# A gated linear recurrence and an MLP in one kernel: blocks of four chunks, a token permutation by DMA, wider FF1 products, a new program order

## The chip, the cores and the metric

The kernel runs on one core of a Trainium2 chip. The metric is the device time of one execution in microseconds; the median of three runs of the kernel before is 198.5 us (196.85 to 198.63).

## The reference

A recurrence over 768 tokens, for 4 batches and 8 heads of 48 channels, followed by an MLP whose activation is h cos(h):

```python
# q, k, v, alpha: (4, 8, 768, 48) f32;  w_in: (384, 2048), w_out: (2048, 384) f32
for t in range(S):
    state = alpha[:, :, t, :, None] * state + np.einsum('bhd,bhe->bhde', k[:, :, t], v[:, :, t])
    y[:, :, t] = np.einsum('bhd,bhde->bhe', q[:, :, t], state)
x = y.transpose(0, 2, 1, 3).reshape(B * S, H * D)      # 3072 x 384
h = x @ w_in
out = (h * np.cos(h)) @ w_out                           # 3072 x 384 f32
```

## The kernel before

The 3072 tokens are 24 chunks of 128, six to a batch; a token is a partition. For a chunk `j`, the logarithms of alpha (`ln`, ACT, L144) are summed along the tokens by a product with a triangular matrix (`cums`, PE, L157), four small products give the sums of the whole chunk (L161), and two exponentials give the decay of each token from the chunk's start and its inverse (`exps`, ACT, L175, L177). These work on pairs of chunks, except for the first two. k is multiplied by the inverse decay (`khat`, POOL, L185), q by the decay (`qhat`, POOL, L191), v is cast (`vcast`, POOL, L195). k and q go, transposed, into the scores (`scores`, PE, L235), which are masked (`mask_scores`, DVE, L244). The transposes are made on PE for the first 8 chunks (`transposes`, L218, evicted by DVE, L224), and by a transposing DMA from SBUF to SBUF for the others (L211). The state is a product of k and v (`state`, PE, L260), to which DVE adds the former state (L272) and which POOL multiplies by the chunk's decay (L274, into `ub`). `outputs` (L289, L292) adds q times state and scores times v; DVE evicts y as bf16 (`ev_outputs`, L299); `x_transposes` turns it, on PE for 6 chunks (L313) and by a transposing DMA for the rest (L307).

The MLP works on one chunk and half of the 2048 hidden channels at a time: FF1 (`ff1`, L330) is 8 x 3 products of 128 x 128 x 128 into a PSUM tile of two banks; ACT takes the cosine as a shifted sine (`act`, L338), DVE multiplies (`gate`, L344), FF2 (`ff2`, L352) adds 2 x 8 products with 384 columns, ACT evicts (L357) and sends the result out on its own DMA queue. `warmup` (L368) issues products of zeros.

All loads and all transposing DMAs are issued by SP, in program order. A load is one chunk of one tensor: 8 heads x 128 tokens, 192 bytes contiguous each (L100, L104). The weights come in quarters of 768 KB (L111, L124), and are cast by DVE and ACT (L117, L115). PSUM has three double-bank buffers (`big`, for sums, scores and FF1), one bank `g` (transposes, state, outputs) and one bank `o` (FF2).

The scheduler is off: a string `ORDER` of 678 units is the program, and each engine takes its instructions in that order. A unit is a letter and a chunk, for example `v0 b0 a0 a1 i0 c0 k0 d0`.

Of the kernel before, what the change touches and what calls it, by code (L numbers as in the profile page):

```python
# [9 lines left out]
FP = mybir.dt.float32  # L10
BF = mybir.dt.bfloat16
# [5 lines left out]
def kernel(  # L17
# [17 lines left out]
    NF = DF // C  # L35
    HF = NF // 2
    HD = H * D
    TD = 8
    QB = 6
    XD = 6  # L40
    CW = HD + NP
    ACOL = [(h % 2) * NP + h // 2 for h in range(H)]
    PF = 6

    consts = ctx.enter_context(tc.tile_pool(name="consts", bufs=1))
    apool = ctx.enter_context(tc.tile_pool(name="apool", bufs=4))
    inpool = ctx.enter_context(tc.tile_pool(name="inpool", bufs=PF))
    cpool = ctx.enter_context(tc.tile_pool(name="cpool", bufs=4))
# [3 lines left out]

# [6 lines left out]
    triu_bf = consts.tile([C, C], BF, tag="triu_bf")  # L59
    make_upper_triangular(nc, triu_bf, 1.0, diag=True)  # L60
    ones_bf = consts.tile([C, 1], BF, tag="ones_bf")
    nc.vector.memset(ones_bf, 1.0)
    halfpi = consts.tile([C, 1], FP, tag="halfpi")
    nc.vector.memset(halfpi, math.pi / 2.0)
    lnab = consts.tile([C, 2, 2, H, 64], BF, tag="lnab")
    nc.vector.memset(lnab, 0.0)
    ident_bf = consts.tile([C, C], BF, tag="ident_bf")
    make_identity(nc, ident_bf)
    kqb = consts.tile([C, 3, 2, H, 64], BF, tag="kqb")
    nc.vector.memset(kqb, 0.0)  # L70
    khb, qhb = kqb[:, :, 0], kqb[:, :, 1]


    vpb = consts.tile([C, 3, H, D], BF, tag="vpb")

    ub = consts.tile([C, 3, NP, 96], BF, tag="ub")
    nc.vector.memset(ub, 0.0)
    mask_f = consts.tile([C, C], FP, tag="mask_f")
    make_upper_triangular(nc, mask_f, 1.0, diag=True)
# [3 lines left out]
    nc.vector.memset(m2[64:128, 1:2], 1.0)  # L83

    w1f = consts.tile([C, 3, DF], FP, tag="w1f")
    w1 = consts.tile([C, 3, DF], BF, tag="w1")
    w2f = consts.tile([C, NF, DM], FP, tag="w2f")
    w2 = consts.tile([C, NF, DM], BF, tag="w2")

    a_t, q_t, k_t, v_t, cp_t, icp_t = {}, {}, {}, {}, {}, {}  # L90

    def rows(t, j):
        b, c = j // NC, j % NC
        return t[b, :, c * C : (c + 1) * C, :].rearrange("h s d -> s h d")

    def load_a(j):
        if j % 2 == 0:
            a_new = apool.tile([C, 2, H, D], FP, tag="a_sb")
            a_t[j // 2] = a_new
        nc.sync.dma_start(out=a_t[j // 2][:, j % 2], in_=rows(alpha, j))  # L100

    def load(nm, src, d, j):
        t = inpool.tile([C, H, D], FP, tag=nm)
        nc.sync.dma_start(out=t, in_=rows(src, j))  # L104
        d[j] = t

    QF = DF // 4

    def load_w1(h):
        f = slice(h * QF, (h + 1) * QF)  # L110
        nc.sync.dma_start(out=w1f[:, :, f], in_=moe_w_in[:, f].rearrange("(k p) f -> p k f", p=C))  # L111
# [7 lines left out]
    def cast_w1(h, eng, k0, k1):  # L119
        f = slice(h * QF, (h + 1) * QF)  # L120
        cast(eng, w1[:, k0:k1, f], w1f[:, k0:k1, f])

    def load_w2(h):
        nc.sync.dma_start(  # L124
            out=w2f[:, 4 * h : 4 * h + 4],
            in_=moe_w_out[4 * h * C : (4 * h + 4) * C, :].rearrange("(f p) n -> p f n", p=C),
        )

    def cast_w2(h):
        cast((nc.vector, nc.scalar)[h % 2], w2[:, 4 * h : 4 * h + 4], w2f[:, 4 * h : 4 * h + 4])  # L130

# [8 lines left out]
    def ln(j0, n):  # L140
        lnset()
        g = j0 // 2
        lo = j0 % 2
        nc.scalar.activation(  # L144
            out=lnab[:, g % 2, lo : lo + n, :, 0:D], in_=a_t[g][:, lo : lo + n], func=AF.Ln
        )

    cum_ps = {}

    def cums(j0, n):  # L150
        g = j0 // 2
        lo = j0 % 2
        if lo == 0 or n == 2:
            cum_new = ps.tile([C, 2, 512], FP, tag="big", bufs=3)
            cum_ps[g] = cum_new
        for i in range(lo, lo + n):
            nc.tensor.matmul(  # L157
                cum_ps[g][:, i, 0:HD], triu_bf, lnab[:, g % 2, i, :, 0:D], start=True, stop=True
            )
            for p in range(NP):  # L160
                nc.tensor.matmul(  # L161
                    cum_ps[g][:, i, HD + p : HD + p + 1],
                    lnab[:, g % 2, i, 2 * p : 2 * p + 2].rearrange("s h d -> s (h d)"),
                    ones_bf, start=True, stop=True,
                )

    def exps(j0, n):
        lnset()
        g = j0 // 2
        lo = j0 % 2  # L170
        if lo == 0 or n == 2:
            cp_new = cpool.tile([C, 2, CW], FP, tag="cpl")
            icp_new = cpool.tile([C, 2, HD], FP, tag="icpl")
            cp_t[g], icp_t[g] = cp_new, icp_new
        nc.scalar.activation(out=icp_t[g][:, lo : lo + n], in_=cum_ps[g][:, lo : lo + n, 0:HD],  # L175
                             func=AF.Exp, scale=-1.0)
        nc.scalar.activation(out=cp_t[g][:, lo : lo + n], in_=cum_ps[g][:, lo : lo + n, 0:CW],  # L177
                             func=AF.Exp, scale=1.0)


    Em_t = {}

    def khat(j):
        icp = icp_t[j // 2][:, j % 2]
        nc.gpsimd.tensor_tensor(out=khb[:, j % 3, :, 0:D], in0=k_t.pop(j),  # L185
                                in1=icp.rearrange("s (h d) -> s h d", h=H), op=ALU.mult)

    def qhat(j):
        cp = cp_t[j // 2][:, j % 2]
        eng = nc.vector if j < 2 else nc.gpsimd  # L190
        eng.tensor_tensor(out=qhb[:, j % 3, :, 0:D], in0=q_t.pop(j),  # L191
                          in1=cp[:, 0:HD].rearrange("s (h d) -> s h d", h=H), op=ALU.mult)

    def vcast(j):
        nc.gpsimd.tensor_copy(out=vpb[:, j % 3, :, 0:D], in_=v_t.pop(j))  # L195

    def emask(j):
        cp = cp_t[j // 2][:, j % 2]
        Em = work.tile([C, NP, 2], FP, tag="Em", bufs=3)
        nc.gpsimd.tensor_tensor(  # L200
            out=Em, in0=cp[:, HD:CW].unsqueeze(2).to_broadcast([C, NP, 2]),
            in1=m2.unsqueeze(1).to_broadcast([C, NP, 2]), op=ALU.mult,
        )
        Em_t[j] = Em

    qkT_ps, qkT_t = {}, {}

    def transposes(j):
        if j >= TD:
            t = work.tile([C, 2 * NP, C], BF, tag="qkT", bufs=QB)  # L210
            nc.sync.dma_start_transpose(out=t, in_=kqb[:, j % 3].rearrange("s i h d -> s (i h d)"))  # L211
            qkT_t[j] = t.rearrange("r b s -> r (b s)")
            return
        t = ps.tile([C, 2 * NP * C], BF, tag="g")
        qkT_ps[j] = t
        for i, src in enumerate((khb, qhb)):
            for p in range(NP):
                nc.tensor.transpose(  # L218
                    t[:, (i * NP + p) * C : (i * NP + p + 1) * C],
                    src[:, j % 3, 2 * p : 2 * p + 2].rearrange("s h d -> s (h d)"), ident_bf)  # L220

    def ev_transposes(j):
        t = work.tile([C, 2 * NP * C], BF, tag="qkT", bufs=QB)
        nc.vector.tensor_copy(out=t, in_=qkT_ps.pop(j))  # L224
        qkT_t[j] = t
# [3 lines left out]
    def scores(j):  # L229
        t = ps.tile([C, H * C], FP, tag="big", bufs=3)  # L230
        A_ps[j] = t
        for h in range(H):
            base = 64 * (h % 2)
            p = h // 2
            nc.tensor.matmul(  # L235
                t[:, ACOL[h] * C : (ACOL[h] + 1) * C],
                qkT_t[j][base : base + D, p * C : (p + 1) * C],
                qkT_t[j][base : base + D, (NP + p) * C : (NP + p + 1) * C],
                start=True, stop=True,
            )  # L240

    def mask_scores(j):
        t = work.tile([C, H * C], BF, tag="A_sb")
        nc.vector.tensor_tensor(  # L244
            out=t.rearrange("s (h t) -> s h t", h=H),
            in0=A_ps.pop(j).rearrange("s (h t) -> s h t", h=H),
            in1=mask_f.unsqueeze(1).to_broadcast([C, H, C]), op=ALU.mult,
        )
        A_t[j] = t
# [6 lines left out]
    def state(j):  # L256
        t = ps.tile([C, 512], FP, tag="g")
        U_ps[j] = t
        for p in range(NP):
            nc.tensor.matmul(  # L260
                t[:, p * 96 : (p + 1) * 96],
                khb[:, j % 3, 2 * p : 2 * p + 2].rearrange("s h d -> s (h d)"),
                vpb[:, j % 3, 2 * p : 2 * p + 2, 0:D], start=True, stop=True,
            )

    def ev_state(j):

        t = U_ps.pop(j)[:, 0 : NP * 96].rearrange("r (p e) -> r p e", p=NP)
        sc = t
        if j % NC != 0:  # L270
            sc = work.tile([C, NP, 96], FP, tag="sc")
            nc.vector.tensor_tensor(out=sc, in0=t, in1=ub[:, us(j - 1), :, 0:96], op=ALU.add)  # L272
        eng = nc.vector if j % NC == 0 else nc.gpsimd
        eng.tensor_tensor(  # L274
# [171 lines left out]
```

## Time and profile before

| | |
|---|---|
| median of three runs | 198.5 us (196.85, 198.50, 198.63) |
| span of the profiled execution, first to last instruction | 195.9 us |
| what lies around the span, against the three times | 1.0 to 2.7 us |
| mean granted TensorE clock | 1.000 |
| PE busy | 176.9 us, of it warm-ups 16.3 |
| FF1 (L330), FF2 (L352) | 70.6 us, 68.8 us |
| DVE, ACT, POOL busy | 123.6, 117.4, 75.4 us |
| DMA | 36.20 MB in 131416 packets, 124736 of them under 512 B |
| HBM read, written | 25.17 MB, 4.72 MB |
| loads of one chunk, issue to landing | 4.3 to 4.6 us |
| transposing DMAs, issue to landing | 3.9 us (x), 4.4 us (k and q) |

The profile is of one execution. Busy times of PE hold the pipeline's tails, so a group's busy time is more than the time that it takes when something follows; in the DMA row of the slices, 9 stands for 90% or more. A DMA share above 1 means that packets overlap on an engine. The windows give busy time by stretch of the span; the chain is the work that ended last, followed back.

### The profile page before, as it was taken

The numbers are of one execution on the slowest core, as the hardware profiler recorded it, in microseconds if no ns is written. First come the engines' busy times: TensorE is split into PE (matmuls) and PEld (weight loads), VectorE is DVE, ScalarE is ACT, GpSimd is POOL, SyncE is SP. The second block draws the span as 40 slices with busy tenths as digits, with TensorE's granted clock in tenths as the row PEclk, the third lists the DMA queues.
The fourth block names the chain that finished last, engine by engine and source line by source line (L and its number), as shares of the span: only waits on it lengthen the run. The fifth ranks groups of instructions, "written<-read, shape, count | busy, mean of one in ns | idle before, by whom it ended". The sixth has DMA issues, their size and how long they took to land.

```text
span 195.9 us, 5535 instructions
## 1 busy us (share of the span) xinstructions
PE 176.9 (90%) x2338; PEld 133.6 (68%) x2342; DVE 123.6 (63%) x147; ACT 117.4 (60%) x133; POOL 75.4 (38%) x116
## 2 busy tenths in 40 slices
PE   0899889899999789999898998997998999999993
PEld 0355448698677578887577776776876976697761
DVE  6164767889827647768726585755973698376720
ACT  2344365577877586456686578796857834344641
POOL 4215654340268328252136471533548605220000
PEclk9999999999999999999999999999999999999999
DMA  6999999999999999999999999999899966913012
GB/s 122 191 187 188 240 264 289 324 348 232 209 228 216 210 169 195 179 174 208 234 173 182 163 239 175 187 173 218 156 196 196 221 143 129 182 45 76 7 40 80
DMA packets 131416, 36.20 MB, mean 185 GB/s; under 512 B 124736, under 2 KB 129856, under 8 KB 131392
## 3 DMA queue, kind: packets, MB, share of 16 engines
q1 hardware_dynamic: 127936, 31.14, 88.8%
q10 hardware_dynamic: 3456, 4.72, 9.3%
q8 instruction: 18, 0.29, 0.7%
q14 instruction: 6, 0.05, 0.1%
HBM read 25.17 MB, written 4.72 MB: 153 GB/s over the span
## 4 chain that ended last, share of the span: by engine, by line
PE 31%; SPq 24%; DMA 21%; DVE 7%; issue 7%; POOL 5%; ACT 3%; ACTq 0%; POOLq 0%; DVEq 0%
PE o_new L352 14%; PE t L330 13%; SPq L104 11%; SPq L100 5%; DMA x<-t 4%; DMA w2f<-in_moe_w_out_dram 4%; DVE g_new L344 4%; DMA t<-in_k_dram 4%; SPq L111 3%; SPq L124 3%; DMA t<-in_v_dram 3%; DMA t<-kqb 3%; DMA a_new<-in_alpha_dram 2%; POOL kqb L185 2%; SPq L211 1%
## 5 line engine op out<-in xcount | busy, mean ns | idle before, releaser
L330 PE MATMUL t<-x,w 128*128 128x128 bf16 x1152 | 70.6, 219 | 2.2 <-DMA x<-t 2.1
L344 DVE TENSOR_TENSOR g_new<-t,c_sb 128x1024 bf16<-128x1024 f32 x48 | 58.1, 1221 | 20.6 <-ACT c_sb L338 20.0
L338 ACT ACTIVATE c_sb<-t,halfpi 128x1024 bf16<-128x1024 f32 x48 | 53.0, 1112 | 29.4 <-PE t L330 26.6
L330 PEld LDWEIGHTS <-w 128*128 128x128 bf16 x1152 | 65.5, 98 | 5.0 <-DMA x<-t 2.4
L352 PE MATMUL o_new<-w,g_new 128*128 128x384 bf16 x384 | 68.8, 326 | 0.1
L352 PEld LDWEIGHTS <-g_new 128*128 128x128 bf16 x384 | 35.2, 97 | 20.2
L244 DVE TENSOR_TENSOR t<-t,mask_f 128x1024 bf16<-128x1024 f32 x24 | 28.7, 1218 | 5.3 <-PE t L235 5.3
L185 POOL TENSOR_TENSOR kqb<-t,icp_new 128x384 bf16<-128x384 f32 x24 | 23.9, 999 | 17.3 <-DMA t<-in_k_dram 15.3
L195 POOL CAST vpb<-t 128x384 bf16<-128x384 f32 x24 | 12.1, 503 | 37.4 <-DMA t<-in_v_dram 37.4
L274 POOL TENSOR_TENSOR ub<-sc,Em 128x384 bf16<-128x384 f32 x16 | 13.6, 852 | 28.9 <-DVE sc L272 28.9
L191 POOL TENSOR_TENSOR kqb<-t,cp_new 128x384 bf16<-128x384 f32 x22 | 21.9, 999 | 5.6 <-DMA t<-in_q_dram 3.0
L299 DVE CAST t<-t 128x384 bf16<-128x384 f32 x24 | 13.3, 553 | 14.3 <-PE t L292 14.2
L357 ACT ACTIVATE o_sb<-o_new 128x384 f32<-128x384 f32 x24 | 11.7, 486 | 17.4 <-PE o_new L352 17.4
L144 ACT ACTIVATE lnab<-a_new 128x768 bf16<-128x768 f32 (+1 forms) x13 | 10.3, 794 | 13.9 <-DMA a_new<-in_alpha_dram 13.9
L368 PE MATMUL w_new<-warm 128*128 128x512 bf16 x56 | 16.3, 410 | 0.2
L272 DVE TENSOR_TENSOR sc<-t,ub 128x384 f32<-128x384 f32 x16 | 8.8, 552 | 8.8 <-PE t L260 8.8
L157 PE MATMUL cum_new<-lnab,triu_bf 128*128 128x384 bf16 x24 | 7.5, 339 | 7.6 <-ACT lnab L144 7.6
L175 ACT ACTIVATE icp_new<-cum_new 128x768 f32<-128x768 f32 (+1 forms) x13 | 9.9, 759 | 5.5 <-PE cum_new L161 4.5
L292 PEld LDWEIGHTS <-t 128*128 128x128 bf16 x192 | 9.7, 96 | 3.9 <-DVE t L244 1.2
L292 PE MATMUL t<-vpb,t 128*128 128x48 bf16 x192 | 11.2, 184 | 0.8 <-DVE t L244 0.4
L137 ACT ACT_TABLE_LOAD x8 | 10.3, 1283 | 2.4 <-ACT o_sb L357 1.6
L161 PEld LDWEIGHTS <-lnab 128*128 128x128 bf16 x96 | 5.5, 98 | 8.6 <-issue 6.8
(43 smaller groups left out, 120.4 us busy)
## 6 DMA issues: line engine op xcount, KB each, us to landing
t<-in_v_dram SPq DMA_DIRECT2D x24, 192.0 KB, 4.6
a_new<-in_alpha_dram SPq DMA_DIRECT2D x24, 192.0 KB, 4.6
t<-in_k_dram SPq DMA_DIRECT2D x24, 192.0 KB, 4.4
t<-in_q_dram SPq DMA_DIRECT2D x24, 192.0 KB, 4.3
out_dram<-o_sb ACTq DMA_DIRECT2D x24, 192.0 KB, 3.3
w1f<-in_moe_w_in_dram SPq DMA_DIRECT2D x4, 768.0 KB, 7.0
w2f<-in_moe_w_out_dram SPq DMA_DIRECT2D x4, 768.0 KB, 9.2
x<-t SPq DMA_TRANSPOSE x18, 3.9
```

Of the source, the lines that this page charges most:

```text
L104: nc.sync.dma_start(out=t, in_=rows(src, j))
L185: nc.gpsimd.tensor_tensor(out=khb[:, j % 3, :, 0:D], in0=k_t.pop(j), in1=icp.rearrange("s (h d) -> s h d", h=H), op=ALU.mult)
L191: eng.tensor_tensor(out=qhb[:, j % 3, :, 0:D], in0=q_t.pop(j), in1=cp[:, 0:HD].rearrange("s (h d) -> s h d", h=H), op=ALU.mult)
L244: nc.vector.tensor_tensor(out=t.rearrange("s (h t) -> s h t", h=H), in0=A_ps.pop(j).rearrange("s (h t) -> s h t", h=H), in1=mask_f.unsquee ...
L274: eng.tensor_tensor(out=ub[:, us(j), :, 0:96].rearrange("r p (a e) -> r p a e", a=2), in0=sc.rearrange("r p (a e) -> r p a e", a=2), in1=E ...
L292: nc.tensor.matmul(t[:, h * D : (h + 1) * D], A_t[j][:, ACOL[h] * C : (ACOL[h] + 1) * C], vpb[:, j % 3, h], start=first, stop=True, skip_g ...
L299: nc.vector.tensor_copy(out=t, in_=y_ps.pop(j)[:, 0:HD])
L330: nc.tensor.matmul(t[:, f], w1[:, kk, ft * C : (ft + 1) * C], x_t[j][:, kk], start=(kk == 0), stop=(kk == 2))
L338: nc.scalar.activation(out=c_sb, in_=h_ps[j, half], func=AF.Sin, bias=halfpi, scale=1.0)
L344: nc.vector.tensor_tensor(out=g_new, in0=h_ps.pop((j, half)), in1=c_t.pop((j, half)), op=ALU.mult)
L352: nc.tensor.matmul(o_ps[j][:, 0:DM], g[:, f], w2[:, half * HF + f], start=(f == 0 and half == 0), stop=(f == HF - 1 and half == 1))
L368: nc.tensor.matmul(w_ps, warm[:, 0:C], warm, start=True, stop=True)
```

## The change

Four chunks are now a block, and there are six blocks. In a block, partition p of chunk c holds four neighbouring tokens: chunk c has the partitions 32c to 32c+31, and a load takes 4 x 48 elements, 768 contiguous bytes, per head and partition. Blocks 1 and 4 lie across two batches, and their loads are two DMAs each. The decays inside a partition's four tokens ("slots") are products of the four alphas (`prods`, `prods2`, `kprod`, `qprod`), and only the product of all four goes through logarithm, triangular sum and exponential: one pass per block of 384 columns. k, q (padded to 64 channels) and v are written in bf16 into `pre`, and `permute` brings one chunk of it into token order, from 32 partitions to 128, by a DMA from SBUF to SBUF on SP. From there on a chunk is as before: a transposing DMA, scores, mask, state, outputs, y, x.

The first block goes another way: alpha, k, q and v are loaded in halves of four heads, all four slots go through logarithm and sums (`ln0`, `cums0`, `exp0`, `hat0`), its k and q are transposed on PE in slot order (`pe_transposes`), and the eviction puts them into token order (`ev_transposes`).

Which engine does what: slot products and hats are on POOL, except for `pr`, `kr` and the k hats of block 1 on DVE; v's cast is on ACT (block 0 on POOL); y is evicted by ACT; both operations on the state are on DVE, the first in PSUM. FF1 works on two chunks and a quarter of the hidden channels: 4 x 3 products of 256 columns (for the first two chunks, two times 128). FF2 takes quarters. x is transposed by PE for four chunks. Weights are staged in the loads' own pool of 12 tiles.

The diff, cut to its core:

```diff
+    R = 4
+    M = C // R
+    blk = ctx.enter_context(tc.tile_pool(name="blk", bufs=12))
...
+    def load(nm, src, b):
+        t = blk_tile((nm, b))
+        c = 0
+        while c < R:
+            j = R * b + c
+            n = min(R - c, NC - j % NC)
+            t0 = (j % NC) * C
+            nc.sync.dma_start(
+                out=t[M * c : M * (c + n)].rearrange("p h i d -> p h (i d)"),
+                in_=src[j // NC, :, t0 : t0 + n * C, :].rearrange("h (p i) d -> p h (i d)", i=R))
+            c += n
...
+    ON_DVE = {("pr", 1), ("kr", 1), ("k", 1)}
+    def prods(b):
+        el("pp", b).tensor_tensor(out=pp[:, :, 0:2], in0=a[:, :, 0::2], in1=a[:, :, 1::2], op=ALU.mult)
+        el("pp", b).tensor_tensor(out=pp[:, :, 2], in0=pp[:, :, 0], in1=pp[:, :, 1], op=ALU.mult)
+    def prods2(b):
+        el("pr", b).tensor_tensor(out=a[:, :, 2], in0=pp[:, :, 0], in1=a[:, :, 2], op=ALU.mult)
+        el("pr", b).tensor_tensor(out=a[:, :, 1], in0=pp[:, :, 1], in1=a[:, :, 1], op=ALU.mult)
+    def ln(b):
+        nc.scalar.activation(out=lnb[:, b % 2, :, 0:D], in_=pp_t[b][:, :, 2], func=AF.Ln)
+    def cums(b):
+        nc.tensor.matmul(t[:, 0, 0:HD], t_incl, x[:, :, 0:D], start=True, stop=True)
+        nc.tensor.matmul(t[:, 1, 0:HD], t_strict, x[:, :, 0:D], start=True, stop=True)
+        for p in range(NP):
+            nc.tensor.matmul(t[:, 1, HD + R * p : HD + R * (p + 1)],
+                             x[:, 2 * p : 2 * p + 2].rearrange("s h d -> s (h d)"), sel_bf, ...)
+    def kprod(b):
+        el("kr", b).tensor_tensor(out=kk[:, :, 0::2], in0=kk[:, :, 0::2], in1=a[:, :, 1::2], op=ALU.mult)
+        el("kr", b).tensor_tensor(out=kk[:, :, 1], in0=kk[:, :, 1], in1=pp[:, :, 1], op=ALU.mult)
+    def qprod(b):
+        el("qp", b).tensor_tensor(out=qq[:, :, 0::2], in0=qq[:, :, 0::2], in1=a[:, :, 0::2], op=ALU.mult)
+        el("qp", b).tensor_tensor(out=qq[:, :, 1::2], in0=qq[:, :, 1::2], in1=pp[:, :, 0::2], op=ALU.mult)
+    def hat(b, nm, off, dk, hf):                       # 2 slots x 384 elements each
+        s = slice(2 * hf, 2 * hf + 2)
+        el(nm, b).tensor_tensor(out=pre[:, b % 2, s, off : off + 64 * H]..., in0=blk_t[nm, b][:, :, s]..., in1=dk..., op=ALU.mult)
+    def vcast(b):
+        cast(nc.scalar if b else nc.gpsimd, pre[:, b % 2, :, VO:NW]..., blk_t["v", b]...)
...
+    def permute(j):
+        t = work.tile([C, NW], BF, tag="nat", bufs=5)
+        lo = KO if b == 0 else 0
+        nc.sync.dma_start(out=t[:, lo:], in_=pre[M * c : M * (c + 1), b % 2, :, lo:])
+    def transposes(j):
+        t = work.tile([C, 2 * NP, C], BF, tag="qkT", bufs=6)
+        nc.sync.dma_start_transpose(out=t, in_=nat_t[j][:, 0:VO])
...
     def ev_state(j):
-            nc.vector.tensor_tensor(out=sc, in0=t, in1=ub[:, us(j - 1), :, 0:96], op=ALU.add)
-        eng = nc.vector if j % NC == 0 else nc.gpsimd
-        eng.tensor_tensor(
+            nc.vector.tensor_tensor(out=t, in0=t, in1=ub[:, us(j - 1)], op=ALU.add)
+        nc.vector.tensor_tensor(
...
     def ev_outputs(j):
-        nc.vector.tensor_copy(out=t, in_=y_ps.pop(j)[:, 0:HD])
+        nc.scalar.activation(out=t, in_=y_ps.pop(j)[:, 0:HD], func=AF.Copy)
...
+    def ff1(g, qt, js=slice(0, 2)):
+        for f in range(FQ):
+            ft = qt * FQ + f
             for kk in range(3):
+                nc.tensor.matmul(t[:, f, js], w1[:, kk, ft * C : (ft + 1) * C], x_t[g][:, js, kk],
                                  start=(kk == 0), stop=(kk == 2))
...
+        g_new = moe.tile([C, FQ, 2, C], BF, tag="g_sb", bufs=9)
```

The new `ORDER` has 634 units. In it M, T and D are `permute`, `transposes` and `x_transposes` of a chunk, A, m, Y, y scores, mask, outputs and their eviction, S and u the state; a, k, q, v with a block's number are loads, z and Z quarters of the weights; pp, pr, kr, qp are slot products, kx, ky, qx, qy halves of the hats, vc v's cast. F and V are FF1 and FF2 of four times the pair's (the chunk's) number plus the quarter. SP's part up to the second group of FF products:

```text
ah1 ah0 vh1 vh0 kh0 kh1 qh0 qh1 a1 M0 z0 M1 z1 M2 z2 z3 Z0 Z1 M3 q1 Z2 Z3 k1 a2 v1 a3 q2
M4 M5 M6 M7 T4 T5 T7 T6 k2 D4 D5 k3 v2 D6 D7 q3 a5 a4 M9 M8 M10 M11 T9 ...
```

PE's part over the same stretch:

```text
... Fa3 S2 V0 Y3 D3 V1 F7 F5 S3 F4 V2 V3 F6 V4 V5 V6 V7 V8 V9 V10 V11 cm2 S4 V12 V13 V14 A4
V15 cm3 A5 Y4 A7 Y5 S6 A6 Y7 Y6 F8 F9 F10 S7 V16 ...
```

## The prediction

> **What bounds the kernel now.** I read the page first, for busy shares and the slices.
>
> ```profile
> PE 176.9 (90%) x2338; PEld 133.6 (68%) x2342; DVE 123.6 (63%) x147; ACT 117.4 (60%) x133; POOL 75.4 (38%) x116
> ...
> DMA  6999999999999999999999999999899966913012
> GB/s 122 191 187 188 240 264 289 324 348 232 209 228 216 210 169 195 179 174 208 234 173 182 163 239 175 187 173 218 156 196 196 221 143 129 182 45 76 7 40 80
> ```
>
> Two things are near full, PE and DMA. Second, the windows, to see which of them binds when (the first from 0 to 64 us and on to the last matmul, the others where the traffic is of one kind; last columns: clock, DMA share, GB/s).
>
> ```profile
> 0.00:64.00 64.00, 55.38 (x672) 38.30 (x676) 41.55 (x60) 36.76 (x43) 27.33 (x46) 1.00 1.13 233
> 64.00:192.50 128.50, 121.48 (x1670) 95.34 (x1666) 82.03 (x88) 80.15 (x89) 48.04 (x70) 1.00 0.94 164
> ...
> 5.00:17.00 12.00, 11.34 (x88) 5.69 (x89) 4.42 (x7) 5.29 (x10) 4.18 (x6) 1.00 1.42 189
> 40.00:44.00 4.00, 4.00 (x79) 3.93 (x77) 3.45 (x6) 2.87 (x4) 1.31 (x2) 1.00 1.07 366
> ```
>
> From 64 us on PE is idle for 128.5 - 121.48 = 7.0 us only: PE is the bound there. Before, its busy time is filled with warm-up matmuls, and the queue of loads is the bound: only 192-byte packets move from 5 to 17 us, at 189 GB/s; mostly weights (1.5 and 2 KB packets) from 40 to 44 us, at 366. Third, the chain that ended last shows the hand-over.
>
> ```profile
> 17.06 1.14 SPq L111
> ...
> 37.56 8.63 DMA w2f<-in_moe_w_out_dram
> 46.21 0.96 DVE w L117
> ...
> 50.71 1.34 PE t L330 x24
> 52.05 2.60 PE o_new L352 x16
> ```
>
> SP's issue and the loads carry it until w2 is there at 46.2 us, then PE. It also gives the net price of the two products without pipeline tails: FF1 1.34/24 = 0.0558 us per 128 columns, FF2 2.60/16 = 0.1625 per 384 columns; on the line between them, 256 columns cost 0.109. Fourth, the two products' share of the second stretch:
>
> ```profile
> 64.00:196.00 132.00, 54.22 (x888) 50.41 (x888) 1.00 0.92 161
> 64.00:196.00 132.00, 57.22 (x320) 29.28 (x320) 1.00 0.92 161
> ```
>
> FF1 888 x 0.0558 = 49.6, FF2 320 x 0.1625 = 52.0, together 101.6. The other 19.9 busy us are attention: 7 pairs of cumulative sums (0.66 each in the timeline) are 4.6, transposes 0.6, and 14.7 remain for some 17 chunks, 0.85 per chunk. The last matmul ends 3.4 us before the span does. The span is 195.9, the median of the runs 198.5: I add 2.6 to a span.
>
> **The change, part by part.**
>
> FF1 on two chunks: 528 matmuls of 256 columns x 0.109 + 96 of 128 x 0.0558 = 62.9 us against 64.3. Almost nothing, since loading weights was hidden already.
>
> Cumulative sums: one pair of 384-column products per four chunks, 2 x 0.1625 + 4 small ones = 0.65, where two pairs cost 1.3; PE transposes shrink from 64 + 18 to 32 + 12; warm-ups from 60 to 32. After the first block this takes some 0.7 us per block off PE.
>
> Loads: 768-byte packets, a fourth as many. No row has this size. At the 192-byte rate (189 GB/s) a block's 786 KB takes 4.2 us, at 366 GB/s 2.15. A packet takes 16 x 192 B/189 GB/s = 16.3 ns and 16 x 1536 B/366 GB/s = 67 ns; on the line between, 38 ns for 768 B, 323 GB/s, 2.43 us. I take 2.43. A batch has six chunks, so blocks 1 and 4 lie in two batches: each of their slots is two DMAs of 64 partitions. No row has 64 partitions either, so their price has the same ends, 2.15 and 4.2; the packets being the same, I take 2.43 again.
>
> Permute (M, from SBUF to SBUF, 24 new DMAs on SP): 360 KB, 1.9 us at 189 GB/s, 1.0 at 366; its packets are 2816 bytes, so 1.0. It reads only 32 partitions. [...]
>
> Slot products on POOL: L185's 384 elements take 0.999 us, the 8-element L200 0.243, so 768 take about 1.85. A block needs 2.85 (pp) + 2.0 (pr) + 2.85 (kr) + 3.7 (qp) + 4 x 1.85 (hats) = 18.8 us. The cover is PE's own block: 4 x 5.22 + 4 x 0.85 + 0.65 = 24.9 us. If it were gone, all 18.8 would stand ahead of the block's first transpose.
>
> ```profile
> L185 POOL TENSOR_TENSOR kqb<-t,icp_new 128x384 bf16<-128x384 f32 x24 | 23.9, 999 | 17.3 <-DMA t<-in_k_dram 15.3
> L244 DVE TENSOR_TENSOR t<-t,mask_f 128x1024 bf16<-128x1024 f32 x24 | 28.7, 1218 | 5.3 <-PE t L235 5.3
> L299 DVE CAST t<-t 128x384 bf16<-128x384 f32 x24 | 13.3, 553 | 14.3 <-PE t L292 14.2
> ```
>
> The y eviction goes from DVE (0.553) to ACT (L357's 0.486), the state's multiplication from POOL (0.852) to DVE (0.556), v's cast to ACT (1.48). Per block: DVE 12 x 1.22 + 8 x 0.555 = 19.1, ACT 8 x 1.11 + 8 x 0.49 + 1.5 + 1.5 + 2.6 (two table loads) = 18.4. Both stay under 24.9, so cost nothing. The state's eviction now holds the single PSUM tile g for two DVE operations instead of one, 0.56 more per chunk; it is covered while FF products stand between S and Y in the order, and shows where they run out, which is next.
>
> **The path to steady state.** FF1 itself starts sooner than now (29.66): w1's first quarter stands behind five slot loads and M0, 0.74 + 2.1 + 12.2 + 0.6 + 2.15 = 17.8, then DVE's cast and the first chunk's Y and y, some 21 us. v0's 192 KB are issued at 0.74 and used at 3.90; less 1.05 us of transfer that is 2.1 of latency. Ahead of the second block's first permute, SP issues eleven slot loads, eight weight pieces (2.15 each) and four M (0.6: 229 KB each). v1 is the ninth slot load: 0.74 + 2.1 + 9 x 2.43 + 17.2 + 2.4 = 44.3. Its cast by ACT ends about 46; M4 is issued then, but a3 and q2 stand before it in the queue: 44.3 + 4.9 + 1.0, M4 lands at 50.2. Then SP issues the four T one after another (median 1.85 us each, 4.4 to landing): T6 starts at 55.8, lands at 60.2. Attention follows behind each T with 0.4 (scores) + 1.22 (mask) + 0.5 (outputs) + 0.49 (y), so T4's chain is through at 57.2 and T6's Y at 62.3. D4 and D5 follow T6 and k2 on SP at 58.3 and 59.7, and land 3.9 later, at 63.6. Everything that PE has by then (F0 to F7, V0 to V15) stands ahead of F8 in the order, 8 x 1.32 + 16 x 0.65 = 21.0 us, and it is spent: F8 waits for D5, at 64 us. S4, which needs M4's data, stands on PE ahead of V12 to V15, so these 2.6 us run after 50.2, in the wait for T. Waiting at T and D on SP are k2, k3 and q3; POOL needs them only after 18 us of work on a2, a3 and q2, so they are not late.
>
> So at 64 us the changed kernel has 21.0 us of FF behind it, and before has 264 x 0.0558 + 64 x 0.1625 = 25.1: 4 us behind, but with eight chunks of attention done instead of six, and cheaper ones to come.
>
> **The sum.** From F8: FF 40 x 1.31 + 80 x 0.65 = 104.4; 16 chunks x 0.85 = 13.6; two cumulative sums 1.3; PE idle 7.0 as now, less 2 of the 4.5 us that L330 waits for x, since half of all slot loads is done by then: 5.0. 64 + 104.4 + 14.9 + 5.0 = 188.3; + 3.4 = 191.7 of span; + 2.6 = **194.3, so 194 us**.
>
> Bounds: loads at 366 GB/s and T and D at their shortest (issues 1.29 and 1.18, landings 3.2 and 2.3) bring F8 to about 58; block 1's four slots and M4 at 189 GB/s (4 x 1.73 + 0.9 = 7.8) to 72. All loads at 189 would be the last rival. Idle in the rest: 3 to 10 us.
>
> [...] In the timeline the first seven warm-ups, after 5.5 us without matmuls, take 3.15 us, 0.45 each, and later ones 0.22 to 0.26, although the granted clock reads 1.00 in both. So an idle stretch may cost 7 x 0.2 = 1.4 us. [...] I take nothing for it: attention's matmuls fall into the wait.
>
> **The rivals.**
>
> *A shorter ramp, 188 us (0.18).* F8 at 58. For it: the rate at 44 us and the fact that SP blocks less with a fourth of the packets. Against: weights fall before it whatever the size of q's packets.
>
> *Half-width transfers bind the ramp, 202 us (0.23).* Place: the split slots a1, q1, k1, v1 of block 1 and its M4, in one SP queue, in order. Price: 7.8 us at 189 GB/s, F8 at 72, and each us by which F8 is later is one at the end; from F8 at 70 on it is slower than now by over 1%. For it: F8 stands behind a chain that before did not have (load, cast, M, T, scores, Y, D) with no FF work left to cover it; T and D land 4 us after issue even behind 192 KB loads. Against: the same queue moved 344 to 366 GB/s in mixed packets.
>
> *Nothing gained, 198.5 (0.15).* F8 at 66 and PE idle of 7 us or more as now: what cumulative sums and transposes give, the ramp takes.
>
> *768 bytes are not faster per byte (0.04).* Eleven loads x 1.75 = 19 us later: 213. Against: 366 GB/s with 1.5 KB.
>
> The forecast itself, 190.5 to 196.5, has 0.40. A measurement of this kernel can tell about 1% from no change. Faster by over 1%: 0.40 + 0.18 = 0.58; within: 0.15; slower: 0.23 + 0.04 = 0.27. The range takes in the ramp at 58 with 3 us idle (186) and the half-width ramp at 72 (202) with one more us idle (203); a chance of about 0.15 stays outside.
>
> **What the profile will show.** Right: slot loads of 768-byte packets at 300 GB/s or more in the first 15 us; FF1 of 256 columns from 21 us; a thin stretch on PE from 48 to 64 us, ended by DMA x<-t; then PE above 95% with some 5 us idle; POOL near 75%. Wrong: F8 past 70; block 1's slots at 4 us each; POOL, not PE, without gaps; FF1 at more than 1.4 us per twelve matmuls.

## The result, and the profile after

The changed kernel takes 242.6 us (median; 240.8 to 244.5) where the kernel before takes 198.4 beside it: a ratio of 1.224, with a 95% interval of 1.214 to 1.234. The forecast was 194, with 186 to 203. The profiled execution took 240.8 us with a span of 238.9. It is read in the order of the prediction. First the page: engines, clock and DMA in 40 slices of 6 us.

```profile
PE 186.9 (78%) x1706; PEld 129.9 (54%) x1706; DVE 125.1 (52%) x148; ACT 107.8 (45%) x145; POOL 89.5 (37%) x72
...
PEclk9987999769876689998985999967999988999999
DMA  6999999998999999998899999899966992102012
GB/s 200 329 236 383 379 227 276 222 206 247 193 171 201 223 302 265 261 179 214 170 229 145 174 231 261 174 206 222 183 116 142 168 133 64 52 33 66 3 40 92
```

PE has fallen from 90% to 78% of a longer span, POOL is far from the 75% that was expected, and the DMA row stays at 8 or 9 from the second slice until 173 us, in more than half of that time at 170 to 235 GB/s. The clock row, 9 throughout before, has dips to 5. So far this says DMA; the windows say when PE stood (start:end, length, busy us of PE, PEld, DVE, ACT, POOL, clock, DMA share, GB/s). The last ends with the last FF2 product; 81.8 is where F8 starts.

```profile
0.00:24.60 24.60, 19.30 (x176) 11.78 (x177) 13.78 (x29) 11.39 (x23) 8.36 (x16) 0.86 0.99 290
24.60:81.80 57.20, 35.40 (x353) 24.41 (x351) 30.84 (x38) 24.42 (x35) 26.43 (x19) 0.83 1.07 230
81.80:235.60 153.80, 132.23 (x1180) 93.68 (x1180) 80.48 (x82) 71.67 (x90) 54.67 (x38) 0.92 0.79 163
```

F8 starts at 81.8 us, not 64, and from there to the end it takes 153.8, not 124.3: the ramp is 18 us too long and the rest 29 us. In the rest PE is idle for 21.6 us, where before had 7.0 in its second stage. The chain (start, length, engine or transfer) over the end of the ramp shows what F8 waited for, from M4 on.

```profile
58.11 6.23 DMA t<-pre
...
64.36 7.69 DMA t<-t
...
77.83 3.94 DMA x_new<-t
...
81.81 6.09 PE t_new L410 x36
```

M4 takes 6.2 us from issue to landing, T 7.7, D 3.9. What M4 itself waited for stands in the timeline of SP (start, issue time) and in ACT's waits (total us, times, longest).

```profile
39.69 7.25 SPq L108 DMA_DIRECT2D t_new<-in_v_dram  x2
```

```profile
ACT pre L133 <- DMA t_new<-in_v_dram: 7.2, 3, 4.2
```

SP issues the two halves of v1 from 39.7 to 46.9 us, with five earlier loads not yet landed. The second half lands at 56.5 us; ACT, whose longest wait (4.2 us) this ends, casts v1 from 56.55 to 58.04, and M4 is issued at 58.11. The chain puts a product of POOL ahead of M4 instead, which needs a2 (landed at 53.1); but that product stands behind M4 in the order, so M4 cannot have waited for it. Each of the following blocks has the links M, T and D again. The list of DMA issues has the durations for the whole execution (size of each, median us from issue to landing).

```profile
t<-pre SPq DMA_DIRECT2D x20, 352.0 KB, 6.7
...
t_new<-in_k_dram SPq DMA_DIRECT2D x6, 384.0 KB, 6.8
...
t_new<-in_k_dram SPq DMA_DIRECT2D x3, 768.0 KB, 5.8
...
t<-t SPq DMA_TRANSPOSE x20, 4.2
x_new<-t SPq DMA_TRANSPOSE x20, 4.2
```

A landing also holds what stands ahead in the queue, so the rows of k do not compare the widths: the six of 384 KB are two half loads of the first block, to 128 partitions, and four half slots to 64 partitions, which take 14.2 and 15.8 us in block 1, with six earlier transfers of SP not yet landed, and 5.2 and 6.4 in block 4, with two and three. The trace's packet records compare them: a 768-byte packet takes a mean of 41 ns where only whole slots run and 65 to 79, by the stretch, where halves run, and M's 2816-byte packets take 229 ns, against 95 for 1792 bytes. Last, PE's groups and waits (the second view again: total us, times, longest).

```profile
L430 PE MATMUL o_new<-w,g_new 128*128 128x384 bf16 x384 | 82.0, 348 | 9.2 <-DVE w L135 4.8
L410 PE MATMUL t_new<-x_new,w 128*128 128x256 bf16 (+1 forms) x624 | 77.9, 281 | 5.4 <-DMA x_new<-t 4.8
```

```profile
POOL t_new L209 <- DMA t_new<-in_q_dram: 29.7, 4, 15.9
...
POOL pp L163 <- DMA t_new<-in_alpha_dram: 17.4, 4, 6.4
PE t L325 <- DMA t<-t: 17.2, 6, 5.4
```

POOL and PE both wait for transfers. FF1 and FF2 together are busy for 159.9 us instead of 139.4, and the clock was granted at half for 52.7 us in 11 stretches (1.0 us before).

Three theories follow. **W**: transfers that touch 32 or 64 adjacent partitions (M, and the slots of blocks 1 and 4) hold the DMA engines for nearly twice as long (a slot's packet up to 79 ns in place of 41). **Q**: one SP queue in order, with M, T, D and the loads behind one another, and a chain of M, T, scores, Y, y, D per block that nothing covers. **K**: PE's clock falls in the gaps, and the products that follow cost double (in the chain twelve FF1 products take 2.56 us at half clock and 1.31 at full clock).

### The profile page after: what moved, and what is told of

The parts are those of the page before. It is cut to its first block, busy times and chain, and to the rows that moved or that the text cites. A ratio compares the mean times of both kernels' runs of the same rounds, so it can differ in the third digit from the quotient of the medians.

```text
span 238.9 us, 4167 instructions
## 1 busy us (share of the span) xinstructions
PE 186.9 (78%) x1706; PEld 129.9 (54%) x1706; DVE 125.1 (52%) x148; ACT 107.8 (45%) x145; POOL 89.5 (37%) x72
## 4 chain that ended last, share of the span: by engine, by line
DMA 46%; PE 32%; SPq 10%; ACT 4%; POOL 3%; issue 3%; ACTq 0%; POOLq 0%
DMA t<-pre 16%; PE t_new L410 14%; PE o_new L430 13%; DMA t<-t 13%; DMA t_new<-in_alpha_dram 11%; DMA x_new<-t 6%; SPq L294 4%; SPq L115 2%; PE t L325 2%; POOL pp L163 2%; SPq L108 1%; ACT pre L133 1%; PE t L371 1%; ACT t L377 1%; SPq L287 1%
## 5 line engine op out<-in xcount | busy, mean ns | idle before, releaser
L430 PE MATMUL o_new<-w,g_new 128*128 128x384 bf16 x384 | 82.0, 348 | 9.2 <-DVE w L135 4.8
L410 PE MATMUL t_new<-x_new,w 128*128 128x256 bf16 (+1 forms) x624 | 77.9, 281 | 5.4 <-DMA x_new<-t 4.8
L422 DVE TENSOR_TENSOR g_new<-t_new,c_sb 128x1024 bf16<-128x1024 f32 x48 | 57.9, 1220 | 37.4 <-ACT c_sb L416 37.1
L416 ACT ACTIVATE c_sb<-t_new,halfpi 128x1024 bf16<-128x1024 f32 x48 | 53.0, 1112 | 38.9 <-PE t_new L410 37.1
L331 DVE TENSOR_TENSOR t<-t,triu_f 128x1024 bf16<-128x1024 f32 x24 | 29.2, 1220 | 32.7 <-PE t L325 32.7
L377 ACT ACTIVATE t<-t 128x384 bf16<-128x384 f32 x24 | 11.8, 490 | 19.3 <-PE t L371 14.9
L209 POOL TENSOR_TENSOR t_new<-t_new 128x768 f32<-128x768 f32 x5 | 9.1, 1813 | 29.7 <-DMA t_new<-in_q_dram 29.7
L214 POOL TENSOR_TENSOR pre<-t_new,cp 128x768 bf16<-128x768 f32 x10 | 18.2, 1834 | 0.2
L214 POOL TENSOR_TENSOR pre<-t_new,icp 128x768 bf16<-128x768 f32 x8 | 14.4, 1813 | 0.2
L371 PE MATMUL t<-t 128*128 128x48 bf16 x192 | 12.0, 189 | 1.9 <-DMA t<-pre 1.3
L204 POOL TENSOR_TENSOR t_new<-t_new 128x768 f32<-128x768 f32 x4 | 7.2, 1808 | 14.3 <-DMA t_new<-in_k_dram 14.3
L445 PE MATMUL w_new<-warm 128*128 128x512 bf16 x32 | 11.5, 494 | 1.2 <-DVE warm L58 1.2
```

What stands on the lines that cost most here:

```text
L214: el(nm, b).tensor_tensor(out=pre[:, b % 2, s, off : off + 64 * H].rearrange("p i (h d) -> p i h d", d=64)[:, :, :, 0:D], in0=blk_t[nm, b] ...
L331: nc.vector.tensor_tensor(out=t.rearrange("s (h t) -> s h t", h=H), in0=A_ps.pop(j).rearrange("s (h t) -> s h t", h=H), in1=triu_f.unsquee ...
L371: nc.tensor.matmul(t[:, h * D : (h + 1) * D], A_t[j][:, ACOL[h] * C : (ACOL[h] + 1) * C], v_n[:, VO + h * D : VO + (h + 1) * D], start=fir ...
L377: nc.scalar.activation(out=t, in_=y_ps.pop(j)[:, 0:HD], func=AF.Copy)
L410: nc.tensor.matmul(t[:, f, js], w1[:, kk, ft * C : (ft + 1) * C], x_t[g][:, js, kk], start=(kk == 0), stop=(kk == 2))
L416: nc.scalar.activation(out=c_sb, in_=h_ps[g, qt], func=AF.Sin, bias=halfpi, scale=1.0)
```

## The experiments

All runs but one build on a stand-in of the changed kernel, s0, in which plain DMAs stand for each transposing one; T and D can then be cut and moved like any other transfer. They all leave out the transposition and the decays. Each ratio is to the kernel before as it was measured beside that run, with medians from 197.8 to 200.2 us.

**The stand-in, and the kernel before with the same edit (s0, b0).** The cut shows T; the exponentials' scale of 0 and the tiles of T and D, which are padded from 128 to 130 columns, are not printed.

```diff
-        nc.sync.dma_start_transpose(out=t, in_=nat_t[j][:, 0:VO])
+        src = nat_t[j][:, 0:VO].rearrange("p (b s) -> p b s", s=C)
+        for b0, b1 in ((0, 3), (3, 6), (6, 8)):                 # D: (0, 2), (2, 3)
+            nc.sync.dma_start(out=t[:, b0:b1, 0:C], in_=src[:, b0:b1])
```

> The changed kernel with a stand-in for each of its 40 transposing DMAs, which is the base of the runs that follow: plain SBUF-to-SBUF DMAs of the same bytes in 256-byte packets (three for a chunk's T, two for its D), in the same places of the order; the exponentials have a scale of 0, so that the values stay small. It leaves out the transposition and the decays, so its output is not the reference's; every engine has the same instructions of the same shapes. All theories expect the time of the changed kernel, 242.6 us, if a transposing DMA costs what a plain one of the same packets does: 236 to 249. Under 236 the transposing DMAs themselves have a part in the loss; what comes after is read against this run, not against 242.6.

> The kernel before with the same stand-ins for its transposing DMAs and with exponentials of scale 0 (transposition and decays left out). Expected 198.4, from 193 to 204. If it loses or gains more than 6 us, the stand-in is not neutral and the two bases are compared only with each other.

s0 takes 242.1 us (ratio to before 1.215, 1.204 to 1.227), b0 205.2 (1.029, 1.024 to 1.035). For the changed kernel the stand-in is neutral in time: F8 starts at 85.5 (81.8) and the rest takes 153.2 (153.8). It is not the same work: the 256-byte packets take a mean of 18.8 ns instead of 28.3, and SP issues 100 transfers for T and D instead of 40, in about the same time (82 us against 80). For before it costs 5.8 us by the ratio, and 205.2 is above the 204 that was allowed, so the stand-ins are compared with each other only. The loss is there without a transposing DMA.

**Each narrow transfer by itself (s1_m128, s2_whole).**

```diff
-        nc.sync.dma_start(out=t[:, lo:], in_=pre[M * c : M * (c + 1), b % 2, :, lo:])
+        nc.sync.dma_start(out=t[:, lo:], in_=pre[:, b % 2, c, lo:])              # s1_m128
...
-            n = min(R - c, NC - j % NC)
-            t0 = (j % NC) * C
+            n = R                                                                # s2_whole
+            t0 = min(j % NC, NC - R) * C
```

> The stand-in of the changed kernel with one edit: M reads one slot of all 128 partitions (704 or 448 bytes of each) instead of four slots of 32 partitions; bytes and number of DMAs stay, the token order is wrong. Theory W (narrow transfers hold the DMA engines: in the changed kernel M's 2816-byte packets took a mean of 229 ns, against 95 ns for 1792-byte ones, 40 us of the 16 engines in all): M's packets get short, 8 to 15 us faster than s0. Theory Q (the single SP queue in order, and the chain M, T, scores, Y, y, D per block, which nothing covers): 0 to 4 us faster. Theory K (TensorE's clock at half after gaps): under 3 us.

> The stand-in with one edit: blocks 1 and 4 load other tokens, so that each slot comes in one DMA of 128 partitions instead of two of 64 (wrong tokens for some chunks, same bytes). In the changed kernel a 768-byte packet of the halves took 65 to 79 ns, of whole slots 41. W: block 1's four slots land 8 to 10 us sooner, F8 starts some 8 us sooner, and the end comes 8 to 12 us sooner. Q: 0 to 3 us, since F8 waits at the end of a chain that SP's waits set. K: under 3 us.

s1_m128: 228.1 us; its times lie from 224.3 to 233.4, so it has no interval and the gain is known to some 5 us only, but all are below s0's 240.4 to 244.0. s2_whole: 231.4 us (1.161, 1.154 to 1.168). Gains of some 14 and of 10.7 us, as W had them and Q and K not. The first expectation was wrong on the packets: M's do not get short, they are 2816 bytes in both (1792 in the first block; not 704 or 448), and it is their mean duration that falls, from 224 to 127 ns. The packets of 768 bytes fall from 53.6 to 42.1 ns in the other. The two act in different stages: whole slots bring F8 from 85.5 to 74.4 and leave the rest (152.1); the wide M brings the rest from 153.2 to 141.6, and F8 to 81.4.

**Both, and the same with other partitions (s3_both, s5_il, s13_ilm_whole).** s3_both has both edits. s5_il and s13_ilm_whole keep 32 source partitions for M, but every fourth; s5_il loads the split slots in fours of every fourth partition, s13_ilm_whole as in s2_whole.

```diff
-        nc.sync.dma_start(out=t[:, lo:], in_=pre[M * c : M * (c + 1), b % 2, :, lo:])
+        nc.sync.dma_start(out=t[:, lo:], in_=pre[c::R, b % 2, :, lo:])           # s5_il, s13_ilm_whole
...
-                out=t[M * c : M * (c + n)].rearrange("p h i d -> p h (i d)"),
+                out=(t[c::R] if split else t).rearrange("p h i d -> p h (i d)"), # s5_il, n = 1 if split
```

> Both edits, M from 128 partitions and block 1's and 4's slots in one DMA each, on the stand-in of the changed kernel (wrong tokens and token order). Singly they gave 228 (scattered, 224 to 233) and 231.4 against 242.1. W: they stand one behind the other on the same path, so the gains nearly add: 217 to 221. If one wait only hides behind the other: 225 to 230. What is left over the 205.2 of the stand-in of before (12 us or more) is then for Q and K.

> The stand-in with the same bytes per partition and as few partitions as in the changed kernel, but others: M reads every fourth partition (c, c+4, c+8 ...; 32 of them), and blocks 1 and 4 are loaded in four DMAs of every fourth partition instead of two of 64 adjacent ones (wrong token order). [...] W by the number of partitions, or by the size of M's packets (2816 bytes, unchanged here): no gain, 238 to 246. Q and K: no gain.

> The kernel of whole slots (231.4), with M reading every fourth partition instead of 32 adjacent ones: the same 32 partitions' worth of 2816-byte packets, the same four slots of each. [...] If the number of partitions decides: 229 to 234, packets above 220 ns.

s3_both: 208.6 us (1.047, 1.035 to 1.058), s5_il 216.7 (1.089, 1.079 to 1.099), s13_ilm_whole 207.7 (1.047, 1.036 to 1.058). The first is below every expectation: together the edits give 33.5 us where they gave 14 and 10.7 singly. The others are below what the number of partitions was to give (238 to 246 and 229 to 234), and settle what "narrow" means. With as few partitions, the same slots and the same packets, the spread M is as fast as the one from 128. This also removes a rival: the M from 128 partitions reads one slot and so needs half of its block's hats only, while the spread M needs all of them, as the changed kernel's does.

| mean ns of a packet | s0 | s1_m128 | s2_whole | s3_both | s5_il | s13_ilm_whole |
|---|---|---|---|---|---|---|
| M, 2816 bytes | 224 | 127 | 237 | 121 | 121 | 122 |
| loads, 768 bytes | 53.6 | 53.7 | 42.1 | 42.0 | 42.2 | 42.2 |
| all packets, us over 16 engines | 191.9 | 176.8 | 172.6 | 153.4 | 152.9 | 153.3 |

In these runs the number of partitions is not what counts (32 of them give 237 ns in s2_whole and 122 in s13_ilm_whole); which ones are touched is. The means hide a spread: a quarter of M's packets take 114 ns or less in s0 and in s13_ilm_whole alike, but the median is 142 against 115, and a quarter take over 311 against over 120. So it is not that each packet is slow; many of them are held up. Two lines of the DMA issues, first of s2_whole, then of s13_ilm_whole, show it at the landing (6.0 us to 3.4):

```profile
t<-pre SPq DMA_DIRECT2D x20, 352.0 KB, 6.0
```

```profile
t<-pre SPq DMA_DIRECT2D x20, 352.0 KB, 3.4
```

M's packets took 224 to 237 ns from 32 adjacent partitions and 121 to 122 from every fourth; the 768-byte packets of the loads took 65 to 79 ns to 64 adjacent ones, in the changed kernel, and 42.2 with every fourth in s5_il. By what mechanism, no run shows. That s5_il stays 8 us above s3_both with the same packet times goes with its four DMAs for each split slot in place of one (24 more issues on SP than s3_both); it was not tried by itself, and its cause is not shown.

**M left out (s6_noM, s7_whole_noM), and M cut to a link (s11_smallM).**

```diff
-        t = work.tile([C, NW], BF, tag="nat", bufs=5)
-        nat_t[j] = t
-        lo = KO if b == 0 else 0
-        nc.sync.dma_start(out=t[:, lo:], in_=pre[M * c : M * (c + 1), b % 2, :, lo:])
+        nat_t[j] = pre[:, b % 2, c]                                              # s6_noM, s7_whole_noM
+        t = work.tile([C, C], BF, tag="nat", bufs=5)                             # s11_smallM, beside it
+        nc.sync.dma_start(out=t, in_=pre[:, b % 2, c, KO : KO + C])
```

> The stand-in with M left out: the products and T read slot c of the 128 partitions of pre directly (wrong token order, 24 DMAs fewer, and a step less in each chain). This is M's whole price. The edit that only widened M gave 228. W: most of M's price was its narrow packets, so 222 to 228. Q: a step of the chain and a wait of SP go for every chunk, so under 220. Pre is then held until the block's last product, which could cost a few us.

> The stand-in with whole slots for blocks 1 and 4 and without M (wrong tokens and token order; what is left of the loads is 41-ns packets of 128 partitions). Without M alone: 209.9; M widened and whole slots: 208.6. [...] If the 208.6 is set by SP's issues of T and D, the waits at y and TensorE's own work, which all stay: 203 to 208.

> The kernel of whole slots, with an M of 32 KB (one 128-column block of k, 256-byte packets) instead of 224 to 352 KB: T's first DMA and the first state product read its copy, everything else reads pre directly (wrong tokens and token order). Number of DMAs, the wait of M, T's and the state's wait for its landing stay; M's 19 us of the 16 DMA engines go. With M wide and full it is 208.6, without M 195.0. If M's bytes on the DMA engines cost the rest: 195 to 200. If its step in the chain and its issue on SP do: 204 to 209.

s6_noM: 209.9 us (205.1 to 211.0, without an interval), some 32 less than s0 and some 18 less than the wide M: more than W had, and what Q had. s7_whole_noM: 195.0 us (0.976, 0.971 to 0.981), below the 203 to 208 for the case that SP's issues, the waits at y and PE's own work set the time. This is close to the forecast's time, in the forecast's steps: F8 at 65.9, and 124.3 us from there. The window of that second stage:

```profile
65.90:190.20 124.30, 123.64 (x1180) 89.40 (x1180) 80.08 (x82) 71.33 (x90) 54.16 (x38) 0.98 0.58 150
```

PE is idle for 0.7 us in it, and the DMA share is 0.58. s11_smallM takes 204.4 us (1.031, 1.022 to 1.040), between the two expectations. In ratios to before, from the wide M (1.047) to the small one it is 1.6% or some 3 us, from there to none (0.976) 5.5% or some 11 us. The intervals of the first two overlap, so the price of the bytes is uncertain; but most of what a wide M still costs is not its bytes, it is that M is there, in the chain and in SP's queue. (Without M a chunk also needs half of its block's hats only; the part of that in the 11 us was not separated.)

**SP's issues (s10_t1, s12_t1_narrow).** One plain DMA for a T and one for a D, instead of three and two; s10_t1 on s3_both, s12_t1_narrow on s0.

```diff
-        for b0, b1 in ((0, 3), (3, 6), (6, 8)):                 # D: (0, 2), (2, 3)
+        for b0, b1 in ((0, 8),):                                # D: (0, 3)
```

> The kernel of both edits, with one plain DMA for a chunk's T instead of three and one for D instead of two: the same bytes and packets, 60 issues fewer on SP (0.63 us each, 38 us of 128). SP's issue time as the rest of the loss: 5 to 10 us faster, 198 to 204. If not: 206 to 210. (The changed kernel's own T and D take 80 us of issue for 40, so between the two.)

> The stand-in of the changed kernel, narrow transfers kept, with one DMA for a chunk's T instead of three and one for D instead of two (60 issues fewer). With wide transfers that gave 8.2 us. If SP's issue is a cost of its own: 232 to 236. If it costs only where the transfers leave SP on the path: 239 to 244.

200.4 us (1.005, 1.000 to 1.009) and 231.9 (1.174, 1.164 to 1.183): 4.2% of before, some 8 us, with the wide transfers and with the narrow ones (the plain difference of the narrow ones is 10.2). So the number of issues for T and D is a cost of its own, whatever the width; that it is SP's time and not the size of each transfer was not separated. The chain of s3_both points to SP (the last issue for four T, and the load that stands behind them):

```profile
91.49 0.63 SPq L298
92.17 5.45 DMA t_new<-in_v_dram
```

**Other queues (s8_loads_act, s9_d_act).** Both on s3_both.

```diff
-            nc.sync.dma_start(
+            (nc.sync if b < 2 else nc.scalar).dma_start(                         # s8_loads_act: load
...
-                nc.sync.dma_start(out=x[:, k0:k1], in_=y[:, k0:k1])
+                nc.scalar.dma_start(out=x[:, k0:k1], in_=y[:, k0:k1])            # s9_d_act: D
```

> The kernel of both edits (208.6), with the loads of blocks 2 to 5 issued by ACT instead of SP, at the same places of the order. In that kernel's chain v3, k4, k5 stand on SP behind twelve issues of T at 0.63 us each, and their landing (5.4 us) is then waited for. Q in its queue form (a load waits behind T and D on SP): 3 to 8 us faster, 200 to 205. If what SP does is not late for anything: 206 to 211; ACT's own issues (some 18 at 0.6 to 1 us) could make it slower by a few us.

> The kernel of both edits, with D issued by ACT, which evicts y itself, instead of SP. In that kernel SP waits 20.9 us in six stretches at D for y, and M, T and loads stand behind it. Q in its wait form: 3 to 8 us faster, 200 to 205. If those waits are cover for nothing: 206 to 211, or slower by what 40 issues of 0.6 us cost on ACT ahead of the f of the next quarter.

227.0 us (1.131, 1.121 to 1.142) and 227.1 (1.136, 1.128 to 1.144): both 18 us slower, where a gain or nothing was expected. ACT takes its units in order too, and it waits for PE (in s3_both 29.7 us for FF2 and 26.9 for FF1). D6 is issued at 77.5 us in s9_d_act, behind f8, f9 and f10, and at 68.9 in s3_both; v3 at 103.6 in s8_loads_act and at 92.2 in s3_both. FF1's wait for x in s9_d_act (4.7 us in s3_both):

```profile
PE t_new L416 <- DMA x_new<-t: 18.2, 6, 4.8
```

So these two runs do not decide how much the single queue costs; they show that this order is written for SP, and that in it ACT's queue does not help, since ACT waits itself.

**The clock (s4_warm).**

```diff
+    WARM_A = {4: 14, 9: 8, 12: 6, 16: 14}
+    WARM_F = {(1, 2): 8, (2, 0): 12, (9, 1): 10}
...
+        for _ in range(WARM_A.get(j, 0)):                       # in scores; in ff1 with WARM_F
+            nc.tensor.matmul(t[:, 0:512], warm[:, 0:C], warm, start=True, stop=True)
```

> The stand-in with 72 products of zeros (128x512) in front of seven units of TensorE that follow a long wait (scores of chunks 4, 9, 12 and 16, and three FF1 units), into the tile that the unit fills next. K (in the changed kernel the granted clock was 0.5 in ten stretches, some 14 us of FF at half speed): 4 to 9 us faster. W and Q: the products run in a wait, so within 3 us of s0, or slower by what sticks out of the wait.

247.2 us (1.239, 1.225 to 1.253), 5 slower. In the profiled executions the clock did rise, from a mean of 0.879 to 0.924, half clock fell from 61.0 to 39.8 us, and FF1 and FF2 from 162.8 to 153.3 busy us. (Over all executions the clocks overlap: 0.879 to 0.914 in s0, 0.904 to 0.924 here.) The 9.5 us did not reach the end. But the added products are not free: in five of the seven places the unit follows the last of them without a gap, so they outlast the wait. K's gain did not come; what the clock costs by itself, without the added products, this run does not tell. In the runs where the transfers get faster, half clock goes by itself: 22.4 us in s3_both, 15.5 in s7_whole_noM. The second stages of s0 and s3_both show that this counts:

```profile
85.50:238.70 153.20, 134.77 (x1180) 93.50 (x1179) 80.73 (x82) 71.88 (x90) 56.09 (x39) 0.92 0.70 162
```

```profile
68.60:202.70 134.10, 127.13 (x1180) 89.49 (x1180) 80.30 (x82) 71.57 (x89) 56.12 (x39) 0.97 0.65 186
```

Of the 19.1 us, 11.5 are idle time of PE (18.4 to 7.0) and 7.6 are busy time of the same products, at a clock of 0.97 in place of 0.92. So part of what the waits cost is paid as slower products behind them.

**The stages of all this** (us; start of F8, and from there to the last FF2 product):

| | forecast | after | s0 | s1_m128 | s2_whole | s12_t1_narrow | s3_both | s10_t1 | s7_whole_noM |
|---|---|---|---|---|---|---|---|---|---|
| F8 | 64 | 81.8 | 85.5 | 81.4 | 74.4 | 80.4 | 68.6 | 68.2 | 65.9 |
| rest | 124.3 | 153.8 | 153.2 | 141.6 | 152.1 | 147.5 | 134.1 | 126.7 | 124.3 |

From 242.1 to 195.0: 33.5 us for M and the split slots on 32 or 64 adjacent partitions, 13.6 more when M is then left out. The 13.6 are not M's alone: with the wide M kept, 60 issues fewer gave 8 us as well (s10_t1). A version that is faster than both kernels and computes the reference does not follow: s7_whole_noM owes its time to a token order that is not restored. M with spread partitions (s13_ilm_whole) would restore the order only if all loads were spread too; s5_il, which spreads those of blocks 1 and 4, is at 216.7.

## Why the prediction was wrong, point by point

**What bounds the kernel.** Right for before; for after PE was taken as the bound from F8 on, and it was not: 21.6 us idle, against 5.0.

**The price of a transfer on part of the partitions: the step that failed.** "The packets being the same, I take 2.43 again", and for M "its packets are 2816 bytes, so 1.0". Packets of the same size are not the same. A slot is 1024 packets over 16 engines: 2.7 us at 42 ns, near the 2.43 taken, but 4.2 to 5.1 at the 65 to 79 ns of the halves. An M is 128 packets: 0.97 us at 121 ns, the 1.0 taken, but 1.83 at 229. The prediction had both upper ends, 4.2 and 1.9 at the 189 GB/s of the 192-byte packets, and decided by the size of the packets. The one for M fits the measured 1.83, the one for a slot is at the lower edge of the measured 4.2 to 5.1. With both transfers on 128 partitions the kernel of the runs is 33.5 us faster, so this step is the larger part of the 48 us between forecast and result. Two signs that the prediction named for being wrong stood for it: F8 past 70 (81.8), and block 1's slots at 4 us each.

**768-byte packets.** Right for whole slots: 42 ns against 38, and 329 GB/s in the second slice. The rival of 213 falls.

**The ramp.** v1 was to land at 44.3; it landed at 56.5, 12 us late, and at 46.9 in s3_both. From there to M4's landing it takes 7.9 us instead of 5.9, and on to F8 17.5 instead of 13.8: M4 took 6.2 us, T4 was issued in 4.5 us and landed in 7.7, where 1.85 and 4.4 were taken from before. With the transfers wide the same queue gives F8 at 68.6. The order of the steps was right, and the wait before F8 is ended by DMA x<-t as said. FF1 started at 24.6 instead of 21.

**The rest: a term that was missing, the second step that failed.** The sum after F8 had FF products, attention and idle, and no M at all; M was priced in the ramp only. But M is a link in each block's chain, and 20 of the 24 have 352 KB: a wide M brought 11.6 us of the 29 in this stage, wide M and whole slots 19.1, and M gone from a kernel with whole slots 27.8 (152.1 to 124.3). M took 36 us of the 16 DMA engines in s0 and 20 in s1_m128. The cover that was named for POOL's work was that of PE's own block, 24.9 us; the prediction did not ask whether a block's vc, M, T, scores, Y, y and D fit into it one after another. In the profile after, vc2 to F16 is 91.1 to 115.6, 24.5 us, and vc2 itself stood behind f11 on ACT.

**Nothing for other engines.** Right: DVE, ACT and POOL are at 52, 45 and 37%; none is the bound. POOL's 75% was a slip of the prediction: it is 18.8 us of 24.9 within a block, but POOL has five such blocks, 94 us, which is 49% of the forecast's own 192 us. In s7_whole_noM, at the forecast's time, POOL is at 48%.

**The clock.** "I take nothing for it: attention's matmuls fall into the wait". That was wrong: half clock rose from 1.0 to 52.7 us. In this trace each of PE's four longest gaps (3.6 to 5.4 us) has a stretch at half clock at its end, but six more such stretches come with shorter gaps only, of 3.0 us at most; the eleventh comes after the last product. Filling gaps gained nothing (s4_warm), and the clock came back when the transfers got faster, so it is taken here as a consequence of the waits; what it cost by itself is open.

**FF1 on two chunks.** Right: twelve products take 1.31 to 1.32 us in the chain where the clock is whole.

**That 124.3 came out.** Partly luck: s7_whole_noM has 0.7 us idle where 5.0 were added, and more busy time than the 119.3 of the sum, its clock being 0.98 and its tails counted. The 5.0 had a weak source besides: the 4.5 us that L330 waits for x add the waits of PE (2.1) and PEld (2.4), which are the same stretches.

**The rivals.** "Half-width transfers bind the ramp, 202" named the right cause and the place of one half of it; it stopped at block 1 and M4, with 7.8 us, and measured they are 17 in the ramp and 19 after it (s0 to s3_both). "The same queue moved 344 to 366 GB/s in mixed packets" was the argument against it, and all of those transfers had 128 partitions. That SP blocks less with a fourth of the packets, an argument for the shorter ramp, held over the whole execution: its issues of the loads of alpha, k, q and v took 45.6 us in place of 88.8.

## What to carry to other kernels

Price a transfer by which partitions it touches, on either side, before its packet size: here 32 or 64 adjacent ones took 1.6 to 1.9 times as long per packet (224 to 237 ns against 121 to 127, 65 to 79 against 42), and every fourth one did not (121 to 122, and 42.2). A new step in a chain that runs once per block belongs into the sum of the steady state, with its landing and with the queue that it stands in, and the chain's length is to be held against the time that covers it. Before a low clock is treated, look for the waits in front of it: here it rose when the transfers went faster (0.92 in s0, 0.97 in s3_both from F8 on), and filling the gaps with products made the kernel 5 us slower.

## What the runs showed of the hardware that was not expected

The same 2816-byte packets took a mean of 121 to 122 ns from every fourth partition and 224 to 237 from 32 adjacent ones, and the 768-byte loads 42 ns or 65 to 79, a ratio of 1.6 to 1.9; a quarter of M's packets took 114 ns or less in both cases. Faster transfers on the two paths gained more together (33.5 us) than singly (14 and 10.7). An issue of a plain SBUF-to-SBUF DMA held SP for 0.63 us in s3_both's chain, and in the changed kernel the two issues of v1 for 7.25 us with five earlier loads not yet landed: 60 issues fewer were worth 8 us with PE at 80% of the span and at 87% alike. The clock was granted at half after gaps of PE of 3.0 us and less, in six of eleven stretches. And 72 added products shortened FF1 and FF2 by 9.5 us, at a granted clock of 0.924 in place of 0.879, without a gain.
